# Retention and a gated feed-forward on one core: slot 5's transposes on the DMA engines in turns with the loads, 10 parts of O ahead of group 2, and a new order of the first stage

## The chip, the cores and the metric

The kernel runs on one core of a Trainium2 chip. The metric is the device time of one execution in microseconds (us); lower is better. TensorE is called PE, VectorE DVE, ScalarE ACT, GpSimd POOL and SyncE SP, as in the profile.

## The reference

```python
state = zeros(B, H, D, D)                       # B, H, S, D = 4, 8, 768, 64
for t in range(S):
    state = gamma[h] * state + k[t] (outer) v[t]
    y[t] = D**-0.5 * q[t] @ state
x = y as (B*S, H*D)                             # 3072 x 512
h = x @ w_in                                    # 512 x 2048
out = (h * cos(h)) @ w_out                      # 2048 x 512, float32
```

A linear attention with a decay for each head (retention), and a feed-forward layer whose gate is h cos(h).

## The kernel before

**Slots.** The time axis is cut in 6 chunks of 128 steps, and two batches are taken together: 12 slots p = 0 to 11, in the order of ORDER. A slot needs the loads of its q, k and v (512 KB each), conversions to bf16 with the decay factors (conv_q, conv_k, conv_v), q and k transposed (qkt), and then on PE: A = K Q^T (a_mm, a_one), masked by DVE (a_mask) into am; and the Y block (y_block), which adds the part from the state (y_inter), the part from A (y_part) and the update of the state (s_part). The Y block can also compute A of the next slot on the quarters of PE that it leaves free (a_rows); from slot 2 on all that is done in quarters of the array. Inside a block the second half of the state and Y matmuls waits for the first through a nop on another engine (told and hop_on). y_copy then writes x^T to xt.

**Transposes.** Up to slot DMA_T - 1 they are PE transposes (t_mm, 16 for a slot) and copies from PSUM by DVE or ACT (t_copy, names eq and ek). From slot DMA_T on they are DMA transposes on the queue of SP (dma_t, names dt), two for a slot.

**Feed-forward.** Two slots form a group g of 512 tokens. An F unit (f_mm, f_cos, f_mul) makes 128 of the 2048 columns of h for the 512 tokens: four matmuls, cos on ACT (f_cos), the product on DVE, into gt. A half unit h (h_mm, h_mul) makes 256 columns for the 256 tokens of one slot. O (o_mm) makes one row of 128 tokens by 512 outputs in four parts of four matmuls; o_out copies it out of PSUM on ACT and o_dma stores it from SP's queue. There are seven PSUM banks for all this, handed out first in, first out (Banks), and an eighth for the state.

**The order of the first stage.** All of slots 0 to 5, slot 6's and 7's conversions and transposes, F and O of group 0, the half units of slots 2 and 3 and all loads up to slot 7 are ops of a planner (Plan): each has a cost, what it must follow, a rank, and the banks it takes; ranks are moved by the table SHIFT and engines fixed by ON. The plan is run at build time with its own estimates of DMA landings and then written out as a fixed order for each engine. The planner's times are no waits: on the chip each instruction waits for its semaphores only, but in the order that was written. "issued" as a condition means only after the other's issue. Loads of the first stage go through POOL's queue in the order of LOADS, each issue costing POOL about 1.2 us. HALF0 says up to which of the 16 F units group 0 is made in half units (slot 0's can start before slot 1 is ready), MERGE from which block on the next slot's A is part of the Y block, SPLIT which masks of slots 0 and 1 go over ACT and POOL.

**Steady state.** From group 2 on a loop over g and s = 0 to 15 is written by hand: F unit s of group g, part s of O of group g - 1; at s = 3 and 11 a Y block for slot 2(g+1) or 2(g+1)+1, followed by the conversions and DMA transposes of the slot two later (conv) and the loads of the slot three later on SP's queue.

```python
            if g > 2 or s > 0:
                o_mm(g - 1, *divmod(s, 4))
            if s % 4 == 3:
                o_out(g - 1, s // 4, "A")
            if p < NP and r == 3:
                block(p)
```

Of the kernel before, what the change touches and what calls it, by code (L numbers as in the profile page):

```python
# [28 lines left out]
class Plan:  # L29
# [24 lines left out]
    def ready(self, op):  # L54
        t = 0.0
        for a in op["after"]:
            kind, a = a if isinstance(a, tuple) else ("done", a)
            if a["start"] is None:
                return None
            t = max(t, a["free"] if kind == "issued" else a["done"] + a["lat"])  # L60
        return t
# [103 lines left out]
HOLD = ""  # L165
SHIFT = {"ml010": 25.5, "mulf0.2": -74.7, "f0.3": 0.3, "cosf0.2": -11.6, "cosf0.3": -2.2, "mulf0.3": -4.9, "f0.2": 2.8, "m011": -20.0, "mulh1.4": -20.5, "m000": 82.7, "cosf0.5": -41.6, "ck21": 45.1, "a31": -124.5, "m100": 2.2, "f0.5": 23.0, "a5": -2.5, "v0": -97.2, "ms110": 6.4, "ml110": -41.8, "cosf0.4": -0.9, "f0.4": -9.8, "mulf0.5": 16.9, "eq51": 13.1, "m110": 64.4, "t20": -21.1, "k5": -46.0, "mulf0.8": 31.6, "yc21": -50.4, "f0.6": 2.1, "f0.7": 55.3, "ek10": -92.1, "w0b": -22.2, "a21": -34.2, "h1.0": 81.4, "cosh2.2": 3.0, "m501": 38.5, "yc30": -23.3, "ml011": -27.8, "mulf0.15": 5.8, "sc5": 79.1, "m201": -81.3, "mulh2.2": -18.0, "oc1": -45.8, "mulf0.14": -66.8, "cq31": -32.2, "mulf0.9": -47.9, "mulf0.6": 5.7, "cosf0.7": -27.8, "a30": -8.1, "cosf0.6": -7.2, "h0.2": -12.1, "eq21": -4.6, "cq51": 3.2, "cq41": 38.6, "f0.14": 23.8, "ek20": -13.4, "yc50": 39.8, "cv51": 23.4, "ek51": 88.5, "mulh2.10": 23.3, "cq70": 8.6, "f0.10": -46.0, "mulf0.13": 1.5, "h1.6": 5.9, "ml100": 20.1, "f0.15": 60.8, "o2.1": -8.1, "h3.10": 31.9, "t51": 14.8, "h3.0": -7.1, "h3.14": 28.8, "cq00": -2.7, "m601": 4.7, "h1.4": 1.8, "eq11": 37.0, "cosf0.12": -60.7, "v6": -26.4, "m400": 17.7, "mulh3.12": 67.0, "w2": 49.4, "sw": -53.6, "cv10": -0.0, "rv00": 14.5, "mulh2.8": 4.5, "ek50": 72.2, "cosf0.11": 2.4, "m101": -34.4, "h2.2": 1.1, "q2": -22.9, "q5": -59.7, "cosh3.14": 19.9, "y3": 19.8, "t40": 30.7, "o2": -0.8, "mulh3.4": -0.3, "cq40": -13.2, "mulh0.2": -29.3, "y5": -35.7, "mulh3.14": -25.5, "h2.12": -50.9, "oc0": -94.2, "a10": 39.9, "ek11": -35.3, "h0.6": 6.9, "eq40": -6.2, "h2.6": 58.1, "rv10": -9.1, "dt71": -1.3, "cosh3.8": -31.0, "cosh0.2": 18.8, "cv70": -67.6, "o3.1": -13.8, "cq60": -11.1, "ck60": 71.1, "m511": 10.9, "sc4": -15.9, "o1.3": -16.8, "m510": 4.5, "k4": 12.5, "h0.4": -9.2, "cq71": 3.6, "mulh3.2": 58.9, "cosh1.2": -26.7, "mulh3.6": -1.4, "cv61": 13.7, "o2.2": -9.8, "q6": -7.4, "o0.2": -7.5, "mulh2.4": 44.5, "mulh2.6": 22.6, "mulh3.10": 16.6, "v5": -53.7, "cq61": 27.8, "o1.1": -27.2, "ck61": 0.2, "m200": -10.8, "cosf0.9": 6.3, "cosh0.4": 11.6, "q4": 78.9, "cosh3.6": -6.8, "h1.2": -87.9, "tq01": 1.8, "oc3": -74.8, "mulh0.0": -16.9, "eq01": 11.2, "t21": 6.2, "ck41": 29.7, "cosh3.4": 9.3, "oc2": 8.6, "m211": 23.9, "cq01": -56.9, "w0a": 17.8, "o1.0": -7.7, "yc01": 2.2, "k7": 54.8, "yc51": -0.7, "cosf0.13": -14.9, "cosh2.10": -36.4, "yc00": 7.1, "cosh1.4": -13.4, "ek00": -8.7, "m611": -13.9, "tk10": -101.4, "mulh0.4": -40.7, "mulf0.10": 15.2, "m600": -35.2, "a00": -17.4, "cosh2.0": -5.5, "m301": 18.6, "rv11": -50.0, "sc0": -52.0, "ek01": -31.6, "cv01": 13.3, "ek21": -3.2, "cosf0.10": 7.2, "v7": -2.1, "ek40": 18.1, "t31": 22.7, "mulh1.6": 0.2, "eq30": -9.4, "y4": 19.2, "tk11": 1.9, "ek31": -26.9, "w3b": 23.5, "cosh2.12": -0.2, "cosh0.6": 4.7, "cosh2.8": -4.4, "cosh3.2": 25.8, "cv60": 2.7, "cosh2.4": -14.4, "v4": -1.1, "mulh2.12": 36.6, "dt61": -8.8, "eq41": -12.5, "mulf0.11": 31.8, "ek41": -0.8, "eq50": 9.1, "a11": -23.9, "yc10": 9.3, "o0.3": 0.3, "dt60": -3.3, "o3.3": 50.5, "mulh2.14": -42.3, "m610": -12.1, "f0.11": -0.6, "s0": 3.1, "cv11": 38.9, "h3.8": -17.4, "yc40": 14.3, "m410": -8.4, "h2.8": -4.0, "m300": 15.8, "o0": -14.6, "cv31": -27.4, "rv01": 0.6, "cosf0.14": 2.4, "cosh2.6": 11.7, "cv50": -6.8, "m010": -1.2, "ms011": -12.0, "f0.13": -5.2, "l8": 5.1, "ck70": 3.2, "t41": 1.0, "o1.2": -2.3, "cv71": 0.5, "tq11": 31.2, "h2.4": -3.6, "mulh0.6": 8.8, "t50": 7.1, "ck31": 42.7, "yc20": -52.3, "m001": -4.7, "y01": 62.0, "y2": 15.3, "f0.12": 20.5, "ms111": 2.0, "mulh1.2": -13.9, "cosh3.10": -49.0, "ck51": -9.0, "h0.0": -0.1, "eq31": 1.4, "eq20": -5.1, "q7": 1.5, "cosh3.0": 6.2, "cosh3.12": 1.5, "cv40": 2.3, "y11": 3.6, "o1": -24.4, "cv00": -1.4, "sc2": -3.2, "m411": 18.0, "m210": -8.1, "v3": 0.0, "eq10": 1.1, "tk01": 22.8, "yc41": -25.6, "cq21": -1.8, "f0.9": -31.4}
ON = {"cv70": "P", "cv00": "D", "cv30": "D", "cv31": "D", "cv60": "D", "cv11": "D", "cv10": "P", "rv01": "D", "sc5": "D", "rv11": "A", "yc20": "D", "sc3": "D", "eq40": "DA", "eq50": "A", "rv00": "A", "yc00": "D", "yc31": "DA", "ek51": "D", "ek11": "DA", "sc4": "D", "ek20": "A", "cv61": "P", "eq01": "DA", "cv51": "D", "ek41": "D", "eq41": "A", "cv20": "P", "yc01": "DA", "eq20": "A", "eq30": "DA", "ek50": "D", "ek00": "D", "sc2": "DA", "yc50": "DA", "yc40": "A", "yc21": "A", "cq21": "D", "ek40": "DA", "cv01": "D", "cv71": "P", "cv21": "P", "ek21": "DA", "cv41": "P", "cq20": "D", "ek10": "DA", "yc30": "A", "ek01": "D"}
HALF0, SPARE, RF, RM, COLD = 8, 1, 50.0, 50.0, 5.2
# [3 lines left out]
def kernel(  # L172
# [19 lines left out]
    NG = NP // 2  # L192
    PRE = 5
    NB = 3
    DMA_T = 6

    ORDER = [0, NC] + [x for x in range(1, NP) if x != NC]
    SWAP = 8
    LATE = NC
# [69 lines left out]

    SRC = {"q": (qf, q), "k": (kf, k), "v": (vf, v)}  # L270

    def load(eng, p, names):
# [4 lines left out]
        for n in names.split():  # L277
            t, src = SRC[n[0].lower()]
            if len(n) == 1:
                t = (qb(p) if n == "Q" else kb(p)) if n in "QK" else t[p % PRE]  # L280
                eng.dma_start(  # L281
# [66 lines left out]
    def dma_t(p, w):  # L348
        n = p % NB
        nc.sync.dma_start_transpose(  # L350
            out=qkt[n][:, w], in_=(qs, ks)[w][n].rearrange("p h b d -> p (h b d)"))

    held = {}
# [70 lines left out]
    def y_first(p, b):  # L424
# [3 lines left out]
        for a in range(HP):  # L428
            for j in range(2):
# [4 lines left out]
                    skip_group_check=True)  # L434

    def after(to, ins):
        tc.add_manual_dep(ins.ins, to.ins.name, mybir.DependencyInfo(
            mybir.DependencyClass.Sync, mybir.DependencyReason.DATA),
            reason="row tiles of PE take turns at a bank")

    def quarters(rows):
# [20 lines left out]
    def hop_on(p):  # L467
        return nc.sync if p <= 4 else nc.gpsimd
# [235 lines left out]
    PL = 6  # L704
# [293 lines left out]
```

## Time and profile before

| | |
|---|---|
| median of 6 runs | 209.22 us (208.74 to 209.28) |
| the profiled execution | 209.19 us, of which 207.40 us are the span of the profile |
| granted clock of PE | 1.0 throughout |
| PE busy | 201.2 us, 97% of the span |
| DVE, ACT, POOL busy | 114.4, 115.2, 73.4 us |
| loads and stores | 32.15 MB, mean 155 GB/s; 240 to 340 GB/s from 20 to 62 us |

The profile gives for each engine the busy time and, for each group of instructions, the line, the operation, out<-in by the tiles' names, the shape, the count and the mean time. The timeline has a row for each run of like instructions: start, duration, engine, line, operation, and in brackets how long the engine stood before it and what released it. The chain of waits is followed back from the last instruction. A letter q behind an engine's name (SPq) is its queue of DMA issues. L361 are the PE transposes, L389 and L399 A, L480, L494 and L508 the parts of the Y block, L590 F units, L611 half units, L635 O, L664 matmuls on a tile of zeros that fill PE before the first F unit.

### The profile page before, as it was taken

The numbers are of one execution on the slowest core, as the hardware profiler recorded it, in microseconds if no ns is written. First come the engines' busy times: TensorE is split into PE (matmuls) and PEld (weight loads), VectorE is DVE, ScalarE is ACT, GpSimd is POOL, SyncE is SP. The second block draws the span as 40 slices with busy tenths as digits, with TensorE's granted clock in tenths as the row PEclk, the third lists the DMA queues.
The fourth block names the chain that finished last, engine by engine and source line by source line (L and its number), as shares of the span: only waits on it lengthen the run. The fifth ranks groups of instructions, "written<-read, shape, count | busy, mean of one in ns | idle before, by whom it ended". The sixth has DMA issues, their size and how long they took to land.

```text
span 207.4 us, 5229 instructions
## 1 busy us (share of the span) xinstructions
PE 201.2 (97%) x2178; PEld 108.5 (52%) x2178; DVE 114.4 (55%) x194; ACT 115.2 (56%) x193; POOL 73.4 (35%) x77
## 2 busy tenths in 40 slices
PE   7889999999999999999999999999999999999994
PEld 2447665868945545445445445445444444444442
DVE  5479898775897457438438448448332343333000
ACT  7567787768865347537537547545555553554120
POOL 8869989799973003304303303300000000000000
PEclk9999999999999999999999999999999999999999
DMA  6999999999998875896775985701101101110212
GB/s 116 178 266 212 309 243 312 256 339 281 342 309 144 195 171 123 221 222 164 177 187 124 156 203 123 201 6 55 51 3 51 51 3 51 51 51 0 106 51 101
DMA packets 58600, 32.15 MB, mean 155 GB/s; under 512 B 47696, under 2 KB 53072, under 8 KB 58576
## 3 DMA queue, kind: packets, MB, share of 16 engines
q0 software_dynamic: 14352, 15.47, 33.8%
q1 hardware_dynamic: 44080, 16.28, 31.4%
q8 instruction: 17, 0.28, 0.6%
q10 hardware_dynamic: 144, 0.07, 0.1%
q14 instruction: 7, 0.06, 0.1%
HBM read 27.26 MB, written 6.29 MB: 162 GB/s over the span
## 4 chain that ended last, share of the span: by engine, by line
PE 90%; DMA 6%; POOL 2%; issue 0%; DVE 0%; POOLq 0%; DVEq 0%
PE bank L635 36%; PE bank L590 30%; PE bank L611 10%; DMA kx<-in_k_dram 4%; PE bank L389 2%; PE bank L361 2%; PE bank L480 2%; DMA qkt<-qs 2%; PE bank L655 2%; PE st_ps L508 2%; PE bank L664 1%; PE bank L494 1%; POOL ks L281 1%; PE bank L431 1%; POOL qs L281 1%; POOL vs L336 1%
## 5 line engine op out<-in xcount | busy, mean ns | idle before, releaser
L598 ACT ACTIVATE cosb<-bank,halfpi 128x512 bf16<-128x512 f32 x96 | 65.5, 689 | 54.9 <-PE bank L590 48.1
L635 PE MATMUL bank<-w_out_sb,gt 128*128 128x512 bf16 x368 | 90.9, 379 | 0.0
L602 DVE TENSOR_TENSOR gt<-bank,cosb 128x512 bf16<-128x512 f32 x72 | 49.0, 689 | 55.9 <-ACT cosb L598 55.8
L590 PE MATMUL bank<-xt,w_in_sb 128*128 128x512 bf16 x288 | 73.2, 379 | 0.0
L635 PEld LDWEIGHTS <-gt 128*128 128x128 bf16 x368 | 35.6, 98 | 42.3
L590 PEld LDWEIGHTS <-w_in_sb 128*128 128x128 bf16 x288 | 27.6, 98 | 32.3
L324 POOL TENSOR_TENSOR qs<-qf,gq 128x512 bf16<-128x512 f32 x18 | 18.5, 1047 | 40.6 <-PE bank L480 23.1
L408 DVE TENSOR_TENSOR am<-bank,mask 128x512 bf16<-128x512 f32 x40 | 24.7, 680 | 4.6 <-PE bank L389 4.6
L313 ACT COPY ob<-bank 128x512 f32<-128x512 f32 (+1 forms) x24 | 14.0, 581 | 16.0 <-PE bank L635 13.9
L611 PE MATMUL bank<-xt,w_in_sb 128*128 128x256 bf16 x192 | 22.3, 273 | 0.0
L611 PEld LDWEIGHTS <-w_in_sb 128*128 128x128 bf16 x192 | 18.5, 98 | 3.1
L619 DVE TENSOR_TENSOR gt<-bank,cosb 128x512 bf16<-128x512 f32 x24 | 16.2, 688 | 5.5 <-ACT cosb L598 5.1
L313 ACT CAST xt<-bank 128x512 bf16<-128x512 f32 x21 | 11.4, 588 | 11.4 <-PE bank L480 10.6
L313 ACT CAST ks<-kf 128x512 bf16<-128x512 f32 x20 | 11.5, 627 | 0.9 <-DMA kf<-in_k_dram 0.9
L331 POOL TENSOR_TENSOR vs<-vf,gk 128x512 bf16<-128x512 f32 x8 | 8.2, 1043 | 9.6 <-DMA vf<-in_v_dram 9.6
L664 PE MATMUL bank<-zero 128*128 128x512 bf16 x34 | 10.2, 431 | 1.1 <-DVE halfpi L680 1.1
L480 PE MATMUL bank<-am,vs 64*64 64x128 bf16 (+1 forms) x320 | 10.3, 206 | 0.1
L281 POOL DMA_DIRECT2D vf<-in_v_dram x8 | 9.4, 1182 | 1.2 <-DVE vs L336 1.1
L336 POOL TENSOR_TENSOR vs<-vf,gk 128x512 bf16<-128x512 f32 x8 | 8.4, 1049 | 2.9 <-PE bank L480 1.8
L389 PE MATMUL bank<-qkt 64*64 64x128 bf16 (+1 forms) x320 | 8.0, 206 | 0.3 <-DMA qkt<-qs 0.3
L315 DVE CAST stb<-st_ps 128x512 bf16<-128x512 f32 x9 | 6.2, 688 | 3.6 <-PE st_ps L508 3.0
L480 PEld LDWEIGHTS <-vs 64*64 64x64 bf16 x320 | 7.8, 107 | 0.5 <-POOLq L528 0.2
(66 smaller groups left out, 131.3 us busy)
## 6 DMA issues: line engine op xcount, KB each, us to landing
out_dram<-ob SPq DMA_DIRECT2D x23, 256.0 KB, 2.6
vf<-in_v_dram POOLq DMA_DIRECT2D x8, 512.0 KB, 11.9
qf<-in_q_dram POOLq DMA_DIRECT2D x6, 512.0 KB, 12.7
kf<-in_k_dram POOLq DMA_DIRECT2D x6, 512.0 KB, 12.1
w_out_sb<-in_moe_w_out_dram POOLq DMA_DIRECT2D x4, 512.0 KB, 13.7
qf<-in_q_dram SPq DMA_DIRECT2D x4, 512.0 KB, 4.4
w_in_sb<-in_moe_w_in_dram POOLq DMA_DIRECT2D x4, 256.0 KB, 8.7
w_in_sb<-in_moe_w_in_dram POOLq DMA_DIRECT2D x2, 512.0 KB, 11.0
```

The costliest lines, as they stand in the source:

```text
L281: eng.dma_start(out=t.rearrange("p b h d -> p (b h) d"), in_=src[ds(2 * bp, 2), :, ds(c * C, C), :].rearrange("b h t d -> t (b h) d"))
L313: nc.scalar.copy(out=out, in_=in_)
L324: ENG[e].tensor_tensor(out=qb(p)[:, b], in0=qf[p % PRE][:, b], in1=bc(gq, ORDER[p] % NC), op=ALU.mult)
L408: nc.vector.tensor_tensor(out=am[p % 2][b][u], in0=bank.rearrange("p (a t) -> p a t", a=HP), in1=(dec[:, b] if p < 2 else mask[second(p, 0 ...
L480: m = nc.tensor.matmul(held["yp", p][b][ts(j, 64), a, lo:], lhsT=vs[p % NB][ts(r, 64), b, h, :], rhs=am[p % 2][b][h // 4][ts(r, 64), h % 4 ...
L590: nc.tensor.matmul(bank, lhsT=w_in_sb[:, i, ts(f, 128)], rhs=xt[g % 2][:, i, :], start=(i == 0), stop=(i == KIN - 1))
L598: nc.scalar.activation(out=cb, in_=bank, func=AF.Sin, bias=halfpi)
L602: nc.vector.tensor_tensor(out=gt[g % 2][:, f, :], in0=bank, in1=cb, op=ALU.mult)
L611: nc.tensor.matmul(bank[:, ts(e, 256)], lhsT=w_in_sb[:, i, ts(f + e, 128)], rhs=xt[g % 2][:, i, ts(hf, 256)], start=(i == 0 and e == 0), s ...
L619: nc.vector.tensor_tensor(out=gt[g % 2][:, f : f + 2, ts(hf, 256)], in0=bank.rearrange("p (f t) -> p f t", f=2), in1=cb.rearrange("p (f t) ...
L635: nc.tensor.matmul(bank, lhsT=gt[g % 2][:, f, ts(j, 128)], rhs=w_out_sb[:, f, :], start=(f == 0), stop=(f == KOUT - 1))
L664: nc.tensor.matmul(bank[:, : 256 * n].rearrange("p (n t) -> p n t", n=n), lhsT=zero[:, :128], rhs=zero.unsqueeze(1).to_broadcast([128, n, ...
```

## The change

- DMA_T goes from 6 to 5: slot 5 is transposed by DMA too. Turns are enforced with added dependencies: the first transpose of slot 5 waits for the landing of v of slot 5, that of slot 6 for k of slot 7; the load of q of slot 6 waits for a nop on SP behind slot 5's second transpose, and that of v of slot 7 for one behind slot 7's.
- The first 10 parts of O of group 1 (ROWS + 1/2 rows) become ops of the plan. Group 2 then has one part at its start, and the other five at s = 3, 7, 8, 9 and 10, so its F units come in runs; its second block stands at s = 10 (its 11th F unit) instead of 11.
- MERGE 4 to 3 (A of slot 4 inside block 3), HALF0 8 to 4, SPLIT and the engine of the nop inside a block (HOP: SP for slots 0 to 3, DVE for 4 and 5, POOL after; before SP to 4, then POOL).
- The loads have a new order: v of slot 0 ahead of k of slot 1, w_in in finer pieces (128, 128, 256, 256, 256, 512 columns) with q2 between, o0 ahead of v2, and all of w_out by q4.
- A half unit in the plan may be set 0.43 us before the landing of its second piece of w_in ("early"; planning only). SHIFT, ON, HOLD and the planner's ranks are all new.

```diff
-                t = max(t, a["free"] if kind == "issued" else a["done"] + a["lat"])
+            t = max(t, a["free"] if kind == "issued" else
+                    a["done"] + a["lat"] - (0.43 if kind == "early" else 0.0))
...
-HOLD = ""
+HOLD = "A"
-HALF0, SPARE, RF, RM, COLD = 8, 1, 50.0, 50.0, 5.2
+HALF0, SPARE, RF, RM, COLD = 4, 0, 30.0, 30.0, 5.2
...
+    ROWS = 2
-    DMA_T = 6
+    DMA_T = 5
+    HOP = "SSSSDDP"
...
     def dma_t(p, w):
         n = p % NB
-        nc.sync.dma_start_transpose(
+        t = nc.sync.dma_start_transpose(
             out=qkt[n][:, w], in_=(qs, ks)[w][n].rearrange("p h b d -> p (h b d)"))
+        if p <= PL + 1:
+            first = ("dt", p) not in held
+            held["dt", p] = t
+            if first and p < PL + 1:
+                after(held["load", *(("v", p) if p < PL else ("k", p + 1))], t)
+            elif not first and p != PL:
+                held["told", "q" if p < PL else "v", p + (p < PL)] = nc.sync.nop(nofuse=True)
+
+    def load_behind(p, n):
+        load(nc.gpsimd, p, n)
+        if ("told", n, p) in held:
+            after(held["told", n, p], held["load", n, p])
...
-        return nc.sync if p <= 4 else nc.gpsimd
+        return {"S": nc.sync, "P": nc.gpsimd, "A": nc.scalar, "D": nc.vector}[HOP[min(p, 6)]]
...
-    MERGE = 4
-    CQ, CD = "P", "DP"
-    SPLIT = {(1, 1, 1), (0, 1, 1)}
-    HM, HCQ, HCV = "q2", "", ""
+    MERGE = 3
+    CQ, CD = "P", "D"
+    SPLIT = {(1, 0, 0), (0, 1, 1)}
+    HM, HCQ, HCV = "k2", "v2", "o2"
...
-    LOADS = ["Q1", "K1", "v0", "v1", "w0a", "w0b", "w1", "w2", "q2", "k2", "w3a", "v2", "w3b", "o0", "q3", "k3", "v3", "o1", "q4", "o2", "k4", "v4", "q5", "k5", "o3", "v5", "q6", "k6", "v6", "q7", "k7", "v7"]
+    LOADS = ["Q1", "v0", "K1", "v1", "w0A", "w0B", "w0b", "w1a", "q2", "w1b", "w2", "k2", "o0", "v2", "w3a", "q3", "w3b", "o1", "k3", "v3", "o2", "o3", "q4", "k4", "v4", "q5", "k5", "v5", "q6", "k6", "v6", "q7", "k7", "v7"]
...
+    for j in range(ROWS + 1):
+        for part in range(4 if j < ROWS else 2):
+            T["o", 4 + j, part] = add("E", 0.865, lambda e, j=j, part=part: o_mm(1, j, part), ...
+        if j < ROWS:
+            add("A", (0.49, 0.585), lambda e, j=j: (o_out(1, j, e), o_dma(1, j)), ...
...
     for g in range(2, NG + 1):
+        units = [divmod(n, 4) for n in range(4 * ROWS + 3 if g == 2 else 0, 16)]
         for s in range(16):
...
+            if g == 2 and s == 0:
+                o_mm(1, ROWS, 2)
             if g < NG:
-                if g == 2 and s == 0:
-                    o_mm(1, 0, 0)
                 f_mm(g, s)
...
+            at_block = s in ((3, 10) if g == 2 else (3, 11))
+            row = None
+            if g > 2 or s in (3, 7, 8, 9, 10):
+                j, part = units.pop(0)
+                o_mm(g - 1, j, part)
+                if part == 3:
+                    row = j
+                    o_out(g - 1, j, "A")
+            if p < NP and at_block:
                 block(p)
+            if row is not None:
+                o_dma(g - 1, row)
...
```

## The prediction

> **What bounds the kernel now.** I read the page first: TensorE (PE) is busy for 97% of the span, and the chain that ended last is 90% PE.
>
> ```profile
> PE 201.2 (97%) x2178; PEld 108.5 (52%) x2178; DVE 114.4 (55%) x194; ACT 115.2 (56%) x193; POOL 73.4 (35%) x77
> ...
> PE 90%; DMA 6%; POOL 2%; issue 0%; DVE 0%; POOLq 0%; DVEq 0%
> ```
>
> Busy need not be useful, so the second view was PE's timeline. Zero-tile fillers (L664) end when the first F starts at 16.83. I then summed the useful work from 16.83 to 204.4, where the last row ends (187.6 us), with the pitches of the chain of waits: 72 F of 0.864, 24 half units of 0.873, 92 parts of O of 0.865, four slots of transposes of 0.89, A of slots 2 to 4, ten Y blocks and the last row. It comes to about 186. So PE has under 2 us of holes after 16.83, and a change can win only by taking work off PE, closing one of the few holes, or starting F earlier. These PE rows carry the pieces that the change touches:
>
> ```profile
> 16.83 1.92 PE L611 MATMUL bank<-xt,w_in_sb 128*128 128x256 bf16 x16
> ...
> 55.59 0.39 PE L361 MATMUL bank<-ident,qs 128*128 128x128 bf16 x4
> ...
> 56.48 1.04 PE L611 MATMUL bank<-xt,w_in_sb 128*128 128x256 bf16 x8
> 57.35 1.03 PE L635 MATMUL bank<-w_out_sb,gt 128*128 128x512 bf16 x4
> 58.31 0.63 PE L389 MATMUL bank<-qkt 64*64 64x128 bf16 x32
> 58.88 3.63 PE L635 MATMUL bank<-w_out_sb,gt 128*128 128x512 bf16 x16
> ...
> 69.28 0.22 PE L389 MATMUL bank<-qkt 64*64 64x128 bf16 x2 [0.34 <-DMA qkt<-qs]
> ...
> 70.39 1.90 PE L635 MATMUL bank<-w_out_sb,gt 128*128 128x512 bf16 x8
> ```
>
> Slot 5's PE transposes run from 55.59 to 56.48; slot 4's separate A from 58.31 to 58.88; and block 5, begun at 68.34, ends at 70.39, 2.05 us instead of the 1.49 of block 4 (62.43 to 63.92), because the DMA transpose of slot 6 lands late. Third, the queue of SP (Q and K of slots 6 and 7) and the chain:
>
> ```profile
> 63.49 1.35 SPq L350 DMA_TRANSPOSE qkt<-ks  x1
> 65.02 3.34 SPq L350 DMA_TRANSPOSE qkt<-qs  x2
> 68.47 1.24 SPq L350 DMA_TRANSPOSE qkt<-ks  x1
> ```
>
> and from the chain of waits in order of time (start, duration, what):
>
> ```profile
> 65.02 4.22 DMA qkt<-qs
> ```
>
> Last, the loads. From 3 to 63 us the DMA engines are full (240 to 340 GB/s from 20 us on). Issue plus time to landing puts v5 at 54.0 (39.96 + 14.0), then q6 55.4, k6 57.0, v6 58.5, q7 60.0, k7 61.5, v7 63.0: 1.5 us a load.
>
> **The change part by part.** The sum is made against the profiled execution, 209.19 us (span 207.40 and 1.79 around it); the median is 209.22.
>
> *Off PE.* Slot 5's 16 transposes go: -0.89. MERGE puts A of slot 4 inside block 3: the separate A (0.57) goes and block 3 grows from 1.32 (46.37 to 47.69) to the 1.49 of a merged block, -0.40. HALF0 makes four half units (0.873) into four full ones (0.864): -0.04. Together -1.33, all where PE has no holes, so it counts in full if PE stays fed. The four qkt copies of slot 5 leave DVE and ACT, which have slack.
>
> *The two new DMA transposes* price no PE time; they price the load queue. They wait for v5 (54.0), SP needs 1.3 us for each, and the load of q6 waits for the nop behind them (56.6). On SP nothing due is queued behind: the first output row was issued at 59.77. Behind the waiting POOL stand k6, v6, q7, k7 and the conversions of slots 5 and 6. A load into an empty queue lands after 4.4 us (q8 from SP) to 6.5 (k0 from POOL), so q6 lands at 61.0 to 63.1 instead of 55.4, k7 four loads later at 67.0 to 69.1, and slot 6's transposes, issued behind k7, at 71.2 to 73.4 (1.3 and 2.9). Block 5 can then run at about 71 to 73, 3 to 5 us later than now.
>
> *What covers it.* Ten parts of O of group 1 now belong to the plan: 8.65 us. Work that PE can do before block 5 was 51.5 us (16.83 to 68.34); now it is 51.5 - 1.33 + 8.65 + 0.87 (the last part of O of group 0) = 59.7, to about 76.5. The cover is 3 to 5 us. Without it, each us of lateness is a us of time. Block 4 needs slot 5's transposes, landed by 54.0 + 2.6 + 2.9 = 59.5; it runs at 62.43 now. The wait of 0.56 in block 5 should vanish unless the fixed order puts it too early: I take -0.56.
>
> *A rule beside a row.* The trace gives 2.7 to 2.9 us for a transpose that has the engines to itself and 4.22 for the one at 65.02, issued as the last loads land and with another behind it. The Trainium skill ("DMA: Bandwidth & Descriptors", Rules for kernel authors) says that a transpose next to ordinary DMAs needs nothing. By that rule the turns buy nothing and merely hold q6 back; the sum would lose nothing but the cover of 3 to 5 us. The same skill ("Advanced Engine Details and Errata", X-Bar Transpose) calls such transposes as fast as regular DMAs at 350 to 400 GB/s; an estimate from that page is 0.7 us for 256 KB, which no row here shows.
>
> *Order of the loads.* v0 goes ahead of K1, and 128 columns of w_in come first. K1 lands at about 13.2 (v0's place) instead of 11.7. From K1 to the Y of slot 1 now takes 4.6 us (11.7 to 16.26), in which DVE also copies xt; without that copy some 4.0, so Y of slot 1 at 17.2 to 17.8, its xt at 18.7 to 19.4. Until then only two half units of slot 0 can run. Finished F work at time t is t - 17.05 to t - 17.65 (18.8 or 19.4 less 1.75); now it is t - 17.2 (16.83 and 0.37 of S). Between 0.15 won and 0.45 lost; the first 128 columns at 15.4 instead of 16.0 could at best win 0.6. I take 0.
>
> *Feeding.* q2 now stands ahead of w1b and w2: w2 lands at about 24.2 and F unit 8 wants it at 24.0; k2, o0 and v2 stand ahead of w3a, so units 12 and 13 wait until 31, with three parts of O, transposes and A of slot 2 between, as the seven banks allow. I bound this by 0 and 1.0 (one F unit or so) and take +0.3.
>
> *Hops.* The nop in blocks 4 and 5 moves from SP and POOL to DVE, behind at most one DVE instruction (0.68), ahead of the masks: 0 to 0.7 each, taken +0.1 in all, since DVE is idle at the start of both blocks now or busy with one conversion. Blocks 6 on keep POOL.
>
> *Group 2.* Five parts of O remain; block 7 comes 11 units after block 6, not 16 steps of two with a block between: 11.0 us instead of 15.46. ACT needs 0.689 per F unit of 0.864, so it keeps pace. SP is tighter: counted from block 6, the load of slot 9's K ends at +12.1 and lands at +15.0 (as at 83.07 to 91.40 plus 2.9 now), but ACT wants it at +13.6. ACT then stands 1.4 us, and the cos of units 11 to 15 are late. PE asks for unit 11's bank again seven units later, 6.05 us after block 7; it is free at about 5.2. Cover 0.85 us: cost 0, with 0 to 0.8 for the range. Slot 8's transposes land at +8.9 for a need at +11. The useful work of this stage is only moved.
>
> *Order of everything else* (SHIFT, ON, HOLD, SPLIT). Its effect is bounded by the holes: 0.5 gained, 1.0 lost, since a fixed order waits wherever a landing misses its due time; the nearest row is the 0.34 of block 5. I take +0.3 for new waits.
>
> Sum: -1.33 - 0.56 + 0 + 0.3 + 0.1 + 0.3 = -1.2; from 209.19 that is 208.0, and from bounds all in my favour 209.19 - 1.33 - 0.56 - 0.6 = 206.7.
>
> **The rivals.**
> *Slower: block 5 is overtaken by its transposes.* Place: the load of q6 behind the nop. If the planned order sets block 5 at 70 and slot 6's transposes land at 73.4, PE stands 3.4 us in the block, minus the 1.33 saved: about 211; deciding point: a wait at block 5 above 1.9 us (1.33 and today's 0.56). For it: the order is static, and the trace shows this very wait now. Against: 8.65 us of ready O parts. 18%, at 210.7.
> *No change: the saving is eaten in the first 35 us*, where the bounds of the start and of feeding add up to 1.45: 209.2 at 10%.
> *More than forecast: F starts earlier too*, no new waits: 206.9 at 20%.
> *The change doesn't do what it says*: the nop follows the issue and not the landing of the transposes, so q6 may start beside them. By the row at 65.02 a transpose then costs 1.4 us more, inside the cover: still the forecast.
>
> **How the numbers follow.** The forecast, 208.0, has 52%. With "more than forecast" that makes 0.72 faster; 0.10 same; 0.18 slower; 0.2% (0.4 us) is about what a measurement of this kernel can tell from no change. The range reaches from all bounds in favour, 206.7, over the no-change case to 209.9, where the slower rival is half paid; what is left out on both sides is some 2 in 10.
>
> **What would show it.** Right: no L361 rows after slot 4; transposes in SP's queue from 54 to 57; a stretch of low GB/s there; 10 parts of O of group 1 ahead of the first F of group 2; the merged block 5 near 1.5 us; block 7 about 11 us after block 6. Wrong: PE idle at L389 in block 4 or 5 for over 1 us; fillers or idle between 17 and 35; PE waiting for a bank after block 7 behind ACT's conversion of slot 9's K.

## Result and the profile after

The changed kernel takes 210.45 us (median of 21 runs, 209.32 to 212.66) against 208.95 of the kernel before (42 runs in the same sessions, 208.02 to 211.61): a ratio of 1.0075, 95% interval 1.0056 to 1.0094. It is slower by 0.75%, where 0.6% faster was predicted. Ratios leave out executions more than 1.5% above the fastest of the same kernel; medians and ranges include them. The profiled execution took 211.52 us, its span 209.7 (before: 209.19 and 207.40), so the span grew by 2.3 us; this execution is 1.1 us above the median.

From the page of the changed kernel: the engines (busy, share of the span, instructions), the clock that was granted to PE in 40 slices of the span, and the shares of the chain of waits.

```profile
PE 202.1 (96%) x2147; PEld 106.9 (51%) x2147; DVE 109.7 (52%) x187; ACT 115.2 (55%) x193; POOL 77.8 (37%) x82
...
PEclk9999999999999999799999999999999999999999
...
PE 58%; DMA 20%; POOL 14%; SPq 4%; issue 1%; ACT 0%; DVE 0%; POOLq 0%; DVEq 0%
```

PE has 31 instructions fewer and yet 0.9 us more busy time. One slice in 40 has a lower clock, the 17th, 84 to 89 us. The chain, which was 90% PE, now lies 20% on DMA and 14% on POOL. Something in the middle of the kernel has come to wait for a transfer. PE's timeline shows where (start, duration, and in brackets the idle time ahead and its releaser). L527 opens a Y block; L654 is O, L630 a half unit, L609 an F unit.

```profile
15.48 1.09 PE L630 MATMUL bank<-xt,w_in_sb 128*128 128x256 bf16 x8
...
76.52 0.22 PE L527 MATMUL st_ps<-vs,ks 64*64 64x64 bf16 x2
...
78.02 1.04 PE L654 MATMUL bank<-w_out_sb,gt 128*128 128x512 bf16 x4
...
83.44 0.22 PE L527 MATMUL st_ps<-vx,kx 64*64 64x64 bf16 x2
...
86.24 0.26 PE L527 MATMUL st_ps<-vx,kx 64*64 64x64 bf16 x1 [1.97 <-POOLq L547]
...
87.77 4.54 PE L609 MATMUL bank<-xt,w_in_sb 128*128 128x512 bf16 x16
...
98.29 0.22 PE L527 MATMUL st_ps<-vs,ks 64*64 64x64 bf16 x2
...
111.05 0.22 PE L527 MATMUL st_ps<-vs,ks 64*64 64x64 bf16 x2
```

**Up to block 6 the change wins.** The first F work starts at 15.48 instead of 16.83. Block 5 runs from 76.52 to 78.02, 1.50 us without a wait. Block 6 starts at 83.44. In the kernel before it started at 78.27, and eight parts of O more now stand ahead of it (8 x 0.865 = 6.92): 85.19 would be no gain, so 1.75 us have been won.

**Between block 6 and block 8 it loses 3.77 us.** Before, these two blocks were 30.76 us apart (78.27 to 109.03); without the eight parts of O that is 23.84, so block 8 was due at 83.44 + 23.84 = 107.28. It starts at 111.05. The sum closes: -1.75 + 3.77 = +2.02, and the rest of the span, 98.65 us behind block 8 instead of 98.37, adds 0.28. Together 2.30.

**What block 6 waits for.** Inside block 6 PE stands 1.97 us for the nop of its hop, in POOL's queue (L547). POOL's own timeline:

```profile
57.43 1.19 POOL L292 DMA_DIRECT2D qf<-in_q_dram  x1 [2.58 <-SPq L371]
...
77.20 1.19 POOL L292 DMA_DIRECT2D vf<-in_v_dram  x1 [7.45 <-SPq L371]
...
86.10 2.03 POOL L347 TENSOR_TENSOR vs<-vf,gk 128x512 bf16<-128x512 f32 x2 [7.71 <-DMA vf<-in_v_dram]
```

The load of v7 is the second of the two turns: POOL stands 7.45 us until SP has issued slot 7's transposes (the nop at L371), and issues the load only at 77.20. It takes 8.7 us to land, among slot 8's loads from SP. POOL then waits for it, to convert slot 7's V, and block 6's nop is queued behind that conversion.

**The idle PE costs a second time, by the clock.** Windows of the changed kernel: the stretch, its length, busy time and instructions of PE, PEld, DVE, ACT and POOL, the granted clock, the DMA engines' share, GB/s.

```profile
84.00:86.00 2.00, 0.27 (x23) 0.15 (x11) 0.09 (x1) 0.13 (x1) 0.00 (x0) 1.00 0.45 99
86.00:87.00 1.00, 0.76 (x41) 0.76 (x44) 0.00 (x0) 0.00 (x0) 0.90 (x1) 0.63 0.47 106
87.00:88.00 1.00, 1.00 (x25) 0.72 (x19) 0.76 (x2) 0.51 (x2) 1.00 (x2) 0.50 0.70 159
88.00:89.00 1.00, 1.00 (x3) 0.30 (x2) 1.00 (x2) 1.00 (x4) 1.00 (x2) 0.50 0.44 99
89.00:90.00 1.00, 1.00 (x5) 0.41 (x4) 1.00 (x3) 0.90 (x3) 1.00 (x2) 0.67 0.57 121
90.00:91.00 1.00, 1.00 (x6) 0.48 (x5) 0.91 (x2) 0.76 (x2) 0.25 (x2) 1.00 0.42 111
```

PE is nearly idle from 84 to 86. Afterwards the granted clock is 0.50 to 0.67 until 90; what the four windows lack to a clock of 1.00 adds up to 1.7 us. The four F units behind the block, from 87.84 to 92.31 in the chain of waits, take 4.47 us instead of 3.46, and the block itself takes 4.4 instead of 1.5, of which 1.97 are the wait. Block 7 starts at 98.29; with the nop elsewhere (first experiment) it starts at 94.56. Not every execution pays this second price: the mean clock of the profiled one is 0.990, three of the 21 others show 0.991 or 0.992, and the rest 0.997 to 1.0.

**A second lateness runs beside it, in SP's queue.** SP's timeline in the changed kernel, slots 6 and 7's transposes and then, slot by slot, the loads and transposes of slots 8 and 9:

```profile
70.03 1.23 SPq L361 DMA_TRANSPOSE qkt<-ks  x1
...
76.92 0.45 SPq L292 DMA_DIRECT2D qf<-in_q_dram  x1
77.46 6.17 SPq L300 DMA_DIRECT2D kf<-in_k_dram  x6
83.68 6.01 SPq L300 DMA_DIRECT2D vf<-in_v_dram  x6
...
90.91 1.33 SPq L361 DMA_TRANSPOSE qkt<-ks  x1
...
94.31 5.22 SPq L300 DMA_DIRECT2D kf<-in_k_dram  x6
99.58 5.00 SPq L300 DMA_DIRECT2D vf<-in_v_dram  x6
...
105.77 1.27 SPq L361 DMA_TRANSPOSE qkt<-ks  x1
```

Slot 6's transposes come at 70.03 (before: 63.49), slot 8's loads at 76.92 (70.45), slot 8's K transpose at 90.91 (83.07), slot 9's at 105.77 (97.43). Everything is 6.5 to 8.3 us later, while PE was meant to reach block 8 1.75 us earlier. In the kernel before slot 9's transposes had landed 7.5 us ahead of block 8 (101.5 and 109.03); now they land at about 110.

### The profile page after: what moved, and what is told of

The parts are those of the page before. It is cut to its first block, busy times and chain, and to the rows that moved or that the text cites. A ratio compares the mean times of both kernels' runs of the same rounds, so it can differ in the third digit from the quotient of the medians.

```text
span 209.7 us, 5163 instructions
## 1 busy us (share of the span) xinstructions
PE 202.1 (96%) x2147; PEld 106.9 (51%) x2147; DVE 109.7 (52%) x187; ACT 115.2 (55%) x193; POOL 77.8 (37%) x82
## 4 chain that ended last, share of the span: by engine, by line
PE 58%; DMA 20%; POOL 14%; SPq 4%; issue 1%; ACT 0%; DVE 0%; POOLq 0%; DVEq 0%
PE bank L654 26%; PE bank L609 25%; DMA vf<-in_v_dram 13%; SPq L361 4%; DMA kx<-in_k_dram 4%; DMA kf<-in_k_dram 4%; POOL vs L347 4%; POOL kf L292 2%; POOL qf L292 2%; PE bank L674 2%; POOL vf L292 2%; POOL qs L335 1%; PE bank L499 1%; POOL w_out_sb L316 1%; PE bank L413 1%
## 5 line engine op out<-in xcount | busy, mean ns | idle before, releaser
L617 ACT ACTIVATE cosb<-bank,halfpi 128x512 bf16<-128x512 f32 x96 | 64.5, 688 | 48.7 <-PE bank L609 41.9
L654 PE MATMUL bank<-w_out_sb,gt 128*128 128x512 bf16 x368 | 89.7, 379 | 0.0
L609 PE MATMUL bank<-xt,w_in_sb 128*128 128x512 bf16 x304 | 75.9, 383 | 0.0
L654 PEld LDWEIGHTS <-gt 128*128 128x128 bf16 x368 | 35.5, 98 | 41.5
L609 PEld LDWEIGHTS <-w_in_sb 128*128 128x128 bf16 x304 | 29.2, 99 | 35.4 <-issue 1.4
L335 POOL TENSOR_TENSOR qs<-qf,gq 128x512 bf16<-128x512 f32 x19 | 19.5, 1042 | 21.1 <-DMA qf<-in_q_dram 14.5
L630 PE MATMUL bank<-xt,w_in_sb 128*128 128x256 bf16 x160 | 18.8, 273 | 0.0
L630 PEld LDWEIGHTS <-w_in_sb 128*128 128x128 bf16 x160 | 15.4, 98 | 3.2 <-DMA w_in_sb<-in_moe_w_in_dram 0.2
L347 POOL TENSOR_TENSOR vs<-vf,gk 128x512 bf16<-128x512 f32 x11 | 11.6, 1063 | 10.2 <-DMA vf<-in_v_dram 10.2
L342 POOL TENSOR_TENSOR vs<-vf,gk 128x512 bf16<-128x512 f32 x8 | 8.2, 1042 | 16.4 <-DMA vf<-in_v_dram 16.4
L499 PE MATMUL bank<-am,vs 64*64 64x128 bf16 (+1 forms) x320 | 11.1, 210 | 0.1
L413 PE MATMUL bank<-qkt 64*64 64x64 bf16 (+1 forms) x320 | 9.1, 210 | 0.0
L292 POOL DMA_DIRECT2D qf<-in_q_dram x6 | 7.1, 1176 | 2.6 <-SPq L371 2.6
```

Source lines behind the costliest of these rows:

```text
L292: held["load", n, p] = eng.dma_start(out=t.rearrange("p b h d -> p (b h) d"), in_=src[ds(2 * bp, 2), :, ds(c * C, C), :].rearrange("b h t ...
L335: ENG[e].tensor_tensor(out=qb(p)[:, b], in0=qf[p % PRE][:, b], in1=bc(gq, ORDER[p] % NC), op=ALU.mult)
L347: ENG[e].tensor_tensor(out=vb(p)[:, b], in0=vf[p % PRE][:, b], in1=bc(gk, ORDER[p] % NC), op=ALU.mult)
L499: m = nc.tensor.matmul(held["yp", p][b][ts(j, 64), a, lo:], lhsT=vs[p % NB][ts(r, 64), b, h, :], rhs=am[p % 2][b][h // 4][ts(r, 64), h % 4 ...
L609: nc.tensor.matmul(bank, lhsT=w_in_sb[:, i, ts(f, 128)], rhs=xt[g % 2][:, i, :], start=(i == 0), stop=(i == KIN - 1))
L617: nc.scalar.activation(out=cb, in_=bank, func=AF.Sin, bias=halfpi)
```

## Experiments

Two theories stood against each other. A: all of the loss is the nop of block 6 behind POOL's wait, so taking it off POOL gives the time that was predicted. D: SP's queue is late as well and is the next limit. Two more questions followed: whether the turns or the transposes themselves cause the lateness, and whether the short group 2 alone does.

### The nop of block 6 off POOL

```diff
-    HOP = "SSSSDDP"      ... HOP[min(p, 6)]
+    HOP = "SSSSDDDP"     ... HOP[min(p, 7)]
```

> The changed kernel with one difference: the nop inside block 6 is on DVE instead of POOL (blocks 7 on keep POOL). Theory A (POOL's queue holds block 6: the nop stands behind the conversion of slot 7's V, which waits for a load that landed at 85.9, and PE then runs at a granted clock of 0.50 to 0.67 until 90): the wait of 1.97 us in block 6 goes, block 6 takes about 1.5 us instead of 4.33 and the four F units behind it 3.5 instead of 4.47; time 207.0 to 207.8, ratio to the kernel before 0.990 to 0.995. Rival B (block 6 itself lacks something else that lands at about 86, such as slot 7's transposed K and Q, and the nop is only the last to be named): the wait stays under another name and the time stays near 210.5, ratio 1.007. Rival C (the new order of the first stage loses the time): block 6 starts where it did, at 83.4 in the trace, and less than 1 us is won.

Measured: 211.07 us, ratio 1.0098 (1.0069 to 1.0128). That can't be told from the changed kernel, though its span is 208.8 and the clock stays at 1.0. Blocks 6 and 7 start at 83.47 and 94.56, as due: A's wait was there and has gone. But block 8 starts at 109.91, 2.6 us late. ACT, PE and SP of this run, from their timelines:

```profile
102.14 1.14 ACT L324 CAST ks<-kf 128x512 bf16<-128x512 f32 x2 [4.33 <-DMA kf<-in_k_dram]
```

```profile
95.70 0.24 PE L413 MATMUL bank<-qkt 64*64 64x64 bf16 x2 [0.53 <-DMA qkt<-qs]
...
104.64 1.02 PE L609 MATMUL bank<-xt,w_in_sb 128*128 128x512 bf16 x4 [1.72 <-DVE gt L621]
```

```profile
90.39 1.33 SPq L361 DMA_TRANSPOSE qkt<-ks  x1
...
94.10 6.18 SPq L300 DMA_DIRECT2D kf<-in_k_dram  x6
...
105.45 1.39 SPq L361 DMA_TRANSPOSE qkt<-ks  x1
```

ACT stands 4.33 us for slot 9's K. The cos of F units queue behind that conversion, DVE's products behind the cos, and PE waits 1.72 us for a bank that DVE has not yet freed. Before that, inside block 7, PE waits 0.53 us for slot 8's transposes. The two make 2.25 of the 2.6 us; block 8 itself waits for nothing. SP's times have hardly moved. A is right about the place and wrong about the time; D's wait appears as soon as A's is gone.

### The second turn taken away

```diff
-            elif not first and p != PL:
+            elif not first and p < PL:
```

The load of v7 no longer waits for slot 7's transposes; the nop stays on POOL.

> The changed kernel with one difference: the load of v of slot 7 no longer waits for the nop behind slot 7's DMA transposes; it is issued as soon as POOL comes to it (about 69.8 instead of 77.2). The nop of block 6 stays on POOL. Theory A (POOL's nop is late because of that load): the load lands by about 76 to 78, the conversion is over long before block 6 and the wait there is gone: 207.0 to 208.0, ratio 0.990 to 0.996, unless the transposes of slots 6 and 7, now beside a load, land late for block 5 (76.5), which would cost up to 2 us of it. Rival B (something else holds block 6): the wait stays, ratio about 1.007.

Measured: 211.44 us, 1.0092 (1.0058 to 1.0126). v7 is issued at 70.65 instead of 77.20, POOL converts it at 76.95, and PE has no wait in block 6. So the turn is what held the nop up. The time stays, by the same second wait: SP issues slot 8's K transpose at 90.48 and slot 9's at 106.12, and PE waits for a bank, at 105.28. That group of PE's waits (who waited, for whom, us in all, times, us of one), and the window around it, with the columns of the windows above:

```profile
PE bank L609 <- DVE gt L621: 2.3, 1, 2.3
```

```profile
100.00:110.00 10.00, 7.69 (x36) 3.42 (x35) 4.94 (x8) 6.18 (x11) 2.60 (x3) 1.00 0.76 158
```

After these 2.3 us of idle PE the granted clock stays at 1.00, where it fell after 1.97 us in the changed kernel.

### The nop of block 6 in SP's queue

```diff
-    HOP = "SSSSDDP"      ... HOP[min(p, 6)]
+    HOP = "SSSSDDSP"     ... HOP[min(p, 7)]
```

> The changed kernel with the nop of block 6 on SP. SP issues the 13 loads of slot 8 from 76.9 to 89.7 in the trace of the changed kernel, and the nop stands behind them. Theory A (the queue in which the nop stands decides): PE waits in block 6 until about 89.7 instead of 86.2, so the time grows by some 3 to 4 us over the changed kernel's 210.45, to 213 to 215; a longer slow clock behind it could add 0.5. Rival B (something else holds block 6): no change from 210.5.

Measured: 215.06 us, 1.0294 (1.0265 to 1.0324). From the groups of waits:

```profile
PE st_ps L527 <- SPq L547: 5.0, 1, 5.0
```

The nop now stands behind slot 8's loads in SP's queue, whose last issue ends at 88.40 in this run, and PE goes on at 89.16. It is the queue that a hop stands in that sets its price: 0 on DVE, 1.97 on POOL, 5.0 on SP.

### Slot 5 back on PE's transposes

```diff
-    DMA_T = 5
+    DMA_T = 6
```

with the nop on DVE as in the first experiment.

> The kernel with block 6's nop on DVE, and slot 5 back on PE transposes (DMA_T = 6, so its two DMA transposes and the turn of slot 6's Q go too; the planner orders the stage anew). By the prediction's term 16 transposes of 0.89 us come back on PE: 0.9 us over the kernel with only the nop moved, unless PE has holes there that swallow them (then 0 to 0.4). A rival in which the pause of the loads costs PE time would make this kernel as fast or faster.

Measured: 215.88 us, 1.0318 (1.0289 to 1.0346). Inconclusive: the planner, whose ranks belong to the other setting, writes another order, in which PE is busy for only 8.4 to 8.9 us of each 10 from 60 to 90. The time says nothing on slot 5's transposes alone, but the landings of the loads do. They are in the same order as in the changed kernel, and no DMA transpose stands among them. POOL's conversion of slot 7's Q, which waits for its load (60.15 in the kernel before), in this run and then in the changed kernel:

```profile
62.02 2.49 POOL L335 TENSOR_TENSOR qs<-qf,gq 128x512 bf16<-128x512 f32 x2 [1.26 <-DMA qf<-in_q_dram]
```

```profile
67.71 2.04 POOL L335 TENSOR_TENSOR qs<-qf,gq 128x512 bf16<-128x512 f32 x2 [2.45 <-DMA qf<-in_q_dram]
```

In this run, profiled in an execution of 217.7 us whose clock was 1.00 until 70, k7 lands at 64.0 (issued at 53.51, landed 10.5 us later), 2.5 us later than in the kernel before; in the changed kernel it lands at 69.9. So the new order of the loads explains little of the lateness.

### V of slot 8 issued by POOL instead of SP

```diff
-    add("S", 8.0, lambda e: load(nc.sync, PL + 2, "q ks vs"),
+    add("S", 8.0, lambda e: (load(nc.sync, PL + 2, "q ks"), load(nc.gpsimd, PL + 2, "vs")),
```

Six issues leave SP's queue. First with the nop on DVE, so against the first experiment:

> The kernel with block 6's nop on DVE, and the six loads of slot 8's V issued by POOL (right behind the load of slot 7's V) instead of SP; the order on every engine is otherwise the same. Theory D (after block 6 SP's queue is the bound: the 13 loads of slot 8 start only at 77 because the pause for slot 5 pushed all behind it, and from there SP issues without a hole: loads of slot 8, transposes of slot 8 at 90.4, loads of slot 9, transposes of slot 9 at 105.5, landed at 111 when block 8 wants them): the transposes of slot 8 start 1 to 2 us sooner, those of slot 9 3 to 4 us sooner, and the time falls to 207.0 to 208.5, ratio 0.991 to 0.999. Rival E (the short group 2 itself, or DVE and ACT in it, is the bound): the time stays at 211. Rival F (PE's clock): the time follows the granted clock, which was 1.0 throughout the kernel with the nop on DVE, so it would stay at 211 too.

Measured: 208.89 us, ratio 0.9991 (0.9966 to 1.0017), against 1.0098 without the edit: 2.2 us less, and span 206.4 against 208.8. The profiled execution, 208.18, is one of the quicker ones (207.79 to 209.53, and one of 349.76). SP, PE and ACT of this run, from their timelines:

```profile
89.66 1.26 SPq L361 DMA_TRANSPOSE qkt<-ks  x1
...
93.00 5.49 SPq L300 DMA_DIRECT2D kf<-in_k_dram  x6
...
103.23 1.34 SPq L361 DMA_TRANSPOSE qkt<-ks  x1
```

```profile
107.51 0.22 PE L527 MATMUL st_ps<-vs,ks 64*64 64x64 bf16 x2
```

```profile
99.70 1.17 ACT L324 CAST ks<-kf 128x512 bf16<-128x512 f32 x2 [2.65 <-DMA kf<-in_k_dram]
```

Slot 9's K transpose comes 2.2 us sooner than in the first experiment, ACT waits 1.7 less, PE not at all, and block 8 starts at 107.51, where 107.28 was due. The loss between blocks 6 and 8 is gone, by relief of SP's queue. Theory D holds, with a smaller gain than it forecast: slot 9's transposes were to come 3 to 4 us sooner, and the time was to be 208.5 at most.

The same edit alone, the nop left on POOL:

> The changed kernel with only the second edit: slot 8's V loaded from POOL, the nop of block 6 left on POOL. By theory D with the late POOL nop as a second, separate wait: block 6 waits for slot 7's V as before (until about 86, or longer, since six issues now stand between its load and its conversion), so block 8 can't be earlier than 2.8 to 4 us behind its due time of 107: 210 to 212, no better than the changed kernel. If only SP's queue mattered it would fall like the kernel with both edits, to 207 to 208.5.

Measured: 1.0011 (0.9974 to 1.0048), from six executions of 207.31 to 209.86 us. Five more took 210.53 to 212.56, three of them at a mean clock of 0.991 or 0.992, and one took 349.41 at 0.562. All but that last one have a median of 209.86. So it stays open whether the expected 210 to 212 was missed, and the only profile is of the 349.41, which can't show whether the nop still waits. With the nop on DVE and the same edit POOL's conversion of slot 7's V starts at 85.22, against 86.10 in the changed kernel, so the nop behind it may be held up to 0.9 us less here.

### The first turn taken away

```diff
-            elif not first and p != PL:
+            elif not first and p > PL:
```

with the nop on DVE: the load of q6 does not wait for slot 5's transposes.

> The kernel with block 6's nop on DVE, and the load of slot 6's Q no longer waiting for the nop behind slot 5's transposes; orders the same. Theory D: the loads of slots 6 and 7 start beside slot 5's transposes, K of slot 7 lands 2 to 4 us sooner than 69.9, so slot 6's and 7's transposes and the 13 loads of slot 8 start that much sooner, and block 8 too: 207.5 to 209.5. If transposes beside loads are so slow that the turns are needed, slot 5's land late, but block 4 (68) has over 8 us in hand. Rival E: no change from 211.

Measured: 209.77 us, 1.0046 (1.0022 to 1.0070). DMA issues of this run, then of the changed kernel, in the window from 50 to 66: the transposes of slot 5, us from issue to landing.

```profile
qkt<-qs SPq DMA_TRANSPOSE x1, 7.3
...
qkt<-ks SPq DMA_TRANSPOSE x1, 8.1
```

```profile
qkt<-qs SPq DMA_TRANSPOSE x1, 3.2
...
qkt<-ks SPq DMA_TRANSPOSE x1, 2.8
```

POOL of this run, ahead of and at the load of q6:

```profile
53.78 1.04 POOL L347 TENSOR_TENSOR vs<-vf,gk 128x512 bf16<-128x512 f32 x1 [0.82 <-DMA vf<-in_v_dram]
54.76 1.19 POOL L292 DMA_DIRECT2D qf<-in_q_dram  x1
```

q6 is issued 2.7 us sooner (54.76), and no earlier than that, because in POOL's fixed order it stands behind the conversion of slot 5's V, which waits for the landing of v5 at 53.6. So the pause of the loads gets shorter and does not go: q6 lands at 60.8 instead of 62.6, against 55.4 in the kernel before. The transposes beside the loads take 7.3 and 8.1 us to land instead of 3.2 and 2.8, the four loads from q6 to k7 take 10.1 us instead of 7.3, and k7, expected 2 to 4 us sooner, lands at 71.0 instead of 69.9.

What the loads do without any pause shows in the run with slot 5 back on PE, where POOL issues q6 at 45.52. There q6 lands 1.5 us behind v5 (54.5 to 56.0), as in the kernel before; in the changed kernel it lands 8.9 us behind it (53.7 to 62.6). This pause, which the turn and the order planned around it make, is most of the 8.4 us by which k7 is late. The run is nevertheless 1.3 us faster than the first experiment. Slot 9's K transpose is issued at 104.25 instead of 105.45 and block 8 starts at 108.43 instead of 109.91, so the gain comes through the second wait. Why SP gets there sooner is open.

### Fewer parts of O ahead of group 2

```diff
-    ROWS = 2
+    ROWS = 1
...
-            if g > 2 or s in (3, 7, 8, 9, 10):
+            if g > 2 or s in (3, 5, 6, 7, 8, 9, 10, 12, 14):
```

with the nop on DVE: group 2 is longer, and PE reaches block 6 sooner.

> The kernel with block 6's nop on DVE, and one row of O less ahead of group 2 (6 parts in the plan instead of 10; group 2 gets nine parts, so its blocks stand 13 units apart instead of 11). Theory D: block 8 waits for slot 9's transposes wherever the four parts stand, so no change, 210.5 to 211.5, as long as PE has work until block 5 (four parts less are 3.5 us of its cover; block 5 could then wait up to 1.5 us for slot 6's transposes, hidden by the later wait). Rival E (the short group 2 is the bound by itself): part of the 3.5 us comes back, 208 to 210.

Measured: 210.34 us, 1.0085 (1.0052 to 1.0119), no gain that is clear of the first experiment. Slot 9's K transpose is issued 2.1 us sooner (103.34), block 8 starts at 109.84, where it was 109.91, and block 5 now waits 1.5 us for slot 6's transposes. The expected number came, but not for the expected reason: block 8 no longer waits on slot 9; the other delay is 0.70 us behind block 7, for ACT's copy of xt. The four parts of O are needed ahead of block 5 and behind block 6; moving them moves the wait.

### More issues in SP's queue

V of slot 8 in 12 pieces instead of 6, the same bytes:

```diff
-                    for lo, n4, th in ((0, 4, x), (4, 8, 1 - x), (12, 4, x)):
+                    pieces = ((0, 4, x), (4, 8, 1 - x), (12, 4, x))
+                    if p == 8 and n[0] == "v":
+                        pieces = [(lo + i * n4 // 2, n4 // 2, th) for lo, n4, th in pieces for i in range(2)]
+                    for lo, n4, th in pieces:
```

once with the nop on DVE, once in the kernel before.

> A dose for SP's queue: the kernel with block 6's nop on DVE, and slot 8's V loaded by SP in 12 pieces instead of 6, the same bytes. Theory D (SP issues without a hole from 77 to 111 and block 8 waits for the end of that chain): six more issues of 0.65 us are 3.9 us, and they go into the time one for one, less what the pieces gain by issuing while SP waits: 213 to 215 instead of 211. Rival E (the short group 2 by itself): 211.

> The same dose in the kernel before: slot 8's V in 12 pieces. Theory D: there slot 9's transposes land at about 101.5 and block 8 starts at 109.1, so SP has some 7 us in hand; 3.9 us more on SP change nothing: 208.5 to 209.3, ratio 0.998 to 1.002. If SP's issues cost by themselves (DMA engines, a slower queue), 1 us or more would be lost here too.

Measured: in the changed kernel 213.26 us, 1.0222 (1.0200 to 1.0243), 2.2 us above the first experiment; in the kernel before 209.16, 1.0010 (0.9989 to 1.0031), no difference. SP of the changed kernel with the split; then PE inside its block 7 (L416 is A of slot 8); then SP of the kernel before with the split:

```profile
83.86 8.72 SPq L303 DMA_DIRECT2D vf<-in_v_dram  x12
...
93.79 1.33 SPq L364 DMA_TRANSPOSE qkt<-ks  x1
...
108.12 1.36 SPq L364 DMA_TRANSPOSE qkt<-ks  x1
```

```profile
98.12 0.32 PE L416 MATMUL bank<-qkt 64*64 64x64 bf16 x2 [3.34 <-DMA qkt<-qs]
```

```profile
76.97 8.51 SPq L292 DMA_DIRECT2D vf<-in_v_dram  x12
...
100.90 1.33 SPq L353 DMA_TRANSPOSE qkt<-ks  x1
```

The twelve issues hold SP 3.9 us longer than the six of the first experiment (8.72 against 4.86). Slot 8's K transpose comes 3.4 us later (93.79 against 90.39), and PE waits 3.34 us for slot 8's transposes inside block 7, where it waited 0.53. So the dose acts at block 7 and not, as theory D had it, through slot 9's transposes at block 8. Block 8 starts 3.3 us later (113.24 against 109.91), and the time is 2.2 us longer; a part of that is the clock, granted at 0.50 from 98 to 104 in this run. In the kernel before the split delays slot 9's transposes by 3.5 us (97.43 to 100.90), and nothing waits: 7.5 us of slack were there. With the relief above this is one dose in each direction of SP's queue, and the time follows both, though at different waits.

### More relief

V of slots 8 and 9 by POOL, and in a second kernel of slots 8 to 11, with the nops of blocks 4 and later all on DVE (HOP = "SSSSDDD"). The edit of the first, beside that of slot 8 above:

```diff
-                load(nc.sync, p + 3, "q ks" if at_block else "vs")
+                load(nc.gpsimd if p + 3 == 9 and not at_block else nc.sync, p + 3, "q ks" if at_block else "vs")
```

> The changed kernel with the nops of all blocks from 4 on on DVE, and V of slots 8 and 9 issued by POOL. Theory D: SP is rid of 6 of its issues before slot 8's transposes and 6 before slot 9's, so slot 9's transposes start when its K is converted, about 100 to 101 instead of 105.5, and land before block 8's due time of 107.2; what is left is PE's own work: 206.8 to 208.2, ratio 0.990 to 0.997. Rival: the nops on DVE stand behind the masks and cost PE up to 0.7 us a block, or ACT's wait for slot 9's K goes on, and the time stays at 208.9 as with slot 8 alone.

> The same with V of all slots from 8 to 11 issued by POOL. Theory D: block 8 is met already with slots 8 and 9 moved, later blocks have over 4 us in hand, so no difference from that kernel: within 0.5 us of it, 206.8 to 208.5.

Measured: 210.09 us, 1.0065 (1.0041 to 1.0088), and 211.51 us (209.81 to 214.33), 1.0087 (1.0057 to 1.0116, from the four executions up to 211.51). Both missed: slower than the relief of slot 8 alone. ACT and SP of the first of the two:

```profile
102.29 1.14 ACT L324 CAST ks<-kf 128x512 bf16<-128x512 f32 x2 [3.40 <-DMA kf<-in_k_dram]
```

```profile
94.16 6.25 SPq L300 DMA_DIRECT2D kf<-in_k_dram  x6
...
103.46 1.27 SPq L361 DMA_TRANSPOSE qkt<-ks  x1
```

Slot 9's K is issued no sooner (94.16 to 100.41; 93.00 to 98.49 with slot 8 alone) and ACT waits 3.40 us instead of 2.65, so PE waits 0.8 us for a bank and, inside block 7, 0.7 for slot 8's transposes. A likely reading, which no further run tests: once SP no longer issues slot 9's V, the issue and landing of its K is the limit, which this edit does not touch. Why K's six issues were no quicker is not settled; the nops from block 7 on differ in these two runs as well. No version beat the kernel before: the best, the nop on DVE with slot 8's V on POOL, equals it.

## Why the prediction was wrong

**Off PE and the wait of block 5: right.** No PE transposes follow slot 4's, A of slot 4 is inside block 3 (52.53 to 54.01), block 5 does not wait. These two terms were -1.89; -1.75 was measured at block 6, for all terms up to there together.

**Start, feeding, hops of blocks 4 and 5, new waits of the order: too high by little.** 0.7 us were allowed for them; 0.14 is left of it at block 6. The F work starts 1.35 us earlier, but fillers at 16.41 and 18.34 show that it then waits, as worked out. The sign "fillers or idle between 17 and 35" shows no more than this: one filler, 0.2 us until the next half unit at 18.55, and PE 4.91 us busy from 15 to 20 and 14.99 from 20 to 35.

**Landings: near, one too early.** q6 landed at 62.6 (predicted 61.0 to 63.1) and k7 at 69.9 (67.0 to 69.1). Five loads took 7.5 us before, from the landing of v5 at 54.0 to that of k7 at 61.5; now 16.2, from 53.7 to 69.9. With two transposes among them these loads have taken 8.7 us longer; the prediction allowed 5.5 to 7.6 for k7. Of that 7.4 us lie between v5 and q6, the pause that it had priced, and 1.2 in the four loads behind q6, which took 7.3 us and not the 6.0 of the sum. The cover of block 5 was reckoned rightly against it: slot 6's transposes, issued from 70.03, did not delay it.

**Group 2: the step that failed.** It took SP's times behind block 6 from the old trace: slot 9's K issued by +12.1 and landed at +15.0 ("as at 83.07 to 91.40 plus 2.9 now"), slot 8's transposes landed at +8.9. The old row itself ends at +13.1 (91.40 less 78.27); the prediction gives no reason for the us that it took off. And those offsets belong to a kernel in which slot 8's loads had all been issued 2.6 us after block 6 (78.27 to 80.88). Now they end 6.3 us after it (83.44 to 89.69), slot 9's K is issued by +16.1 and lands at +19.1, slot 8's transposes land at +11.8, for a need at +11. The lateness that had just been worked out for slot 6's transposes was covered at block 5 and then forgotten; SP carried it on to slots 7, 8 and 9. The 8 parts of O that cover it ahead of block 6 were taken from behind it, where they had given SP time. The cost, taken as 0 and bounded at 0.8, was 2.6 us at block 8 with the nop on DVE (109.91, due 107.3). Its wait for a bank behind ACT's conversion of slot 9's K is the one that the prediction had listed as a sign of being wrong: the path was right, the lateness put into it was not. In the changed kernel as profiled this wait does not show, because the next one came first.

**"Blocks 6 on keep POOL": the other part.** The nop stayed where it was, and its price was taken as nothing. But the second turn put a load behind a 7.45 us wait into POOL's queue, the conversion of slot 7's V behind that load, and the nop behind that. The prediction listed what stands behind the waiting q6, and nothing behind the waiting v7. Its price alone is 3.7 us at block 7 in the profiled execution, some 2 of waiting and some 1.7 of lower clock; it shares most of it with the wait in SP's queue, so that taking away either one by the nop or the turn brings nothing (1.0098 and 1.0092 against 1.0075).

**The slower rival: right sign, wrong place.** Its sum, 210.7, is near to the 210.45 measured, but its deciding point, a wait above 1.9 us at block 5, never came. That the number is near is luck.

**The rule weighed there.** The Trainium skill ("DMA: Bandwidth & Descriptors", Rules for kernel authors) has it that a transpose next to ordinary DMAs needs nothing. It stands there as a rule on what must be waited for, beside one on corrupted data, and says nothing of time; that the turns therefore buy nothing was the prediction's own step. Here such transposes landed after 7.3 and 8.1 us instead of 3.2 and 2.8, so the turn does shorten the transposes. The loads behind them came no sooner without it (71.0 against 69.9), so its wait by itself cost the loads nothing; the pause of POOL's order was there in both runs.

## What to carry to other kernels

When a step makes a queue late, follow that lateness through everything behind it in the same queue, up to the place where the queue was idle before; a cover at the first consumer hides the delay and does not remove it. Offsets read from an old trace hold only while the queue that they belong to is as free as it was there. For every enforced wait, list the queue behind it down to the last instruction that another engine needs, a nop included, and when two waits lie side by side, take both away before judging either.

## What the runs showed of the hardware

- Five loads with a pause for two DMA transposes among them took 16.2 us to land, in the same order without pause and transposes 9.5. In a turn of their own the two transposes landed after 3.2 and 2.8 us; issued beside the loads after 7.3 and 8.1, and the four loads from q6 on took 10.1 us instead of 7.3.
- A nop passes once the instruction ahead of it in its queue has been released: PE went on at 86.24, when POOL's conversion, two instructions from 86.10 to 88.13, had only begun.
- After 1.97 us of idle PE the granted clock was 0.50 to 0.67 for nearly 4 us, which cost about 1.7 us more; after 2.31 us in another run it stayed at 1.00, and after 3.34 us it was 0.50 from 98 to 104. The length of the gap alone did not decide it.
- One V of 512 KB in six pieces held SP for 3.9 us (slot 8, kernel before) to 6.0 (slot 8, changed kernel), in twelve for 8.5 to 8.7; POOL issued six pieces in 3.9 us.
